# Reordering the first loads of x and of the Q and K weights in a fused attention-and-MLP kernel, with tile 0 normalised in two parts

## The chip, the cores and the metric

The kernel runs on one core of a Trainium2 chip. The metric is device microseconds of one execution; smaller is better. The profile's span (first to last instruction) is about 1.75 us shorter than that time. Runs of one call share a chip and the executions of the kernel before on it.

## The reference, cut to what matters

```python
xn = _layernorm(x)                      # x: 2048 x 640, bf16
# A: qkv = xn @ wqkv (640 x 1920), 32 heads of 20; each position attends to
#    8 positions at distance 0, 2, ..., 14; output projection wo
# B: ((xn @ w_gate) * (xn @ w_up)) @ w_down, inner width 1536
return x + A(xn, wqkv, wo) + B(xn, w_gate, w_up, w_down)
```

Rows of x are taken in 16 tiles of 128. Nothing can be multiplied before tile 0 is loaded, normalised and transposed, and the first weights are there.

## The kernel before

The kernel is written by a small list scheduler in Python. It is given tasks with priorities, keeps an assumed clock for each engine (with assumed durations and landing times), and so fixes one static order of instructions per engine. On the chip each engine then follows its order and waits for semaphores. A changed assumption about a landing can therefore reorder everything after it. The parts that matter:

```python
    # front(t): one tile of x on VectorE (dve), ScalarE (act), TensorE (pe)
    yield have("x", t)
    if t == 1:
        yield have("sd", 0)             # tile 0's square root has been planned
    for i in range(2):                  # two half-row statistics, 128x320 each
        if t == 2 and i == 1:
            yield have("xnt", 1)
        yield Task("dve", lambda: stats(i), r=[x], prio=-1 if t == 1 and i == 0 else p)
    yield Task("dve", aggr, ...)        # mean and variance
    yield Task("act", sqrt, ...)
    yield Task("dve", recip, ...)
    yield Task("dve" if t < N_DVE_A else "act", apply, ...)  # XNS = (x - mean) * rstd
    # ... transposes on PE into PSUM, then a copy to XNT (tile 0: 3 of 5 row
    # ... blocks copied by dve, 2 by act; tile 0 is followed by 3 warm-up matmuls)

    # projections of tile 0: 12 matmuls with row blocks 0-2 of the weights,
    # 8 with blocks 3-4, for Q and likewise for K; proj_group(...), cut

    x_load(0)
    # ... a small read of wqkv issued by ACT ("touch"), result not used
    x_load(1)
    wqkv_load(0, 0, 3)                  # Q weights, row blocks 0-2 (480 KB)
    wqkv_load(0, 3, NCH)                # Q weights, row blocks 3-4 (320 KB)
    x_load(2)
    wqkv_load(1, 0, 3)                  # K weights, row blocks 0-2
    wqkv_load(1, 3, NCH)                # K weights, row blocks 3-4
    x_load(3)
    warm(18)                            # matmuls on zeros until data is there
```

"Q's first rows" below are row blocks 0 to 2 of the Q weights, "Q's other rows" blocks 3 and 4; likewise for K.

Of the kernel before, what the change touches and what calls it, by code (L numbers as in the profile page):

```python
# [6 lines left out]
ALU = mybir.AluOpType  # L7
# [3 lines left out]
D = 640  # L11
NCH = 5
# [9 lines left out]
TS = 128  # L22
# [27 lines left out]
class Sched:  # L50
# [74 lines left out]
                deps[q.idx] = q  # L125
        return deps

    def op(self, eng, fn, r=(), w=(), dma=False, name="", occ=None, lat=None, lock=False, nbytes=0, mode=0, group=None, extra=0.0, acc=0.0):
        X = _Op()
        X.eng, X.fn, X.name, X.dma, X.group = eng, fn, name, dma, group  # L130
        X.needs_tick, X.event, X.pre_know, X.idx = False, None, None, len(self.ops)
        X.nth = self.n_eng[eng]
        self.n_eng[eng] += 1
        rk = [k for a in r for k in self.keys(a)]
        wk = [k for a in w for k in self.keys(a)]
        deps = self.deps_of(eng, rk, wk)
        if occ is None and not dma:
            occ = 0.1
        inorder = eng in ("pe", "act", "dve")
        start = max([self.t[eng]] + [d.end for d in deps.values()])  # L140
        if lock:
            start = max(start, self.t_lock)
        if eng == "pe" and mode != self.pe_mode:
            start += 0.1
            self.pe_mode = mode
        if dma:
            self.t[eng] = start + (0.48 if occ is None else occ)
            if acc:
                self.t_acc = max(self.t_acc, start + 3.8) + acc
                X.end = self.t_acc  # L150
            else:
                self.t_data = max(self.t_data, start + 1.2) + nbytes / 280e3
                X.end = self.t_data + 0.8 + extra
        else:
            self.t[eng] = start + occ
            X.end = start + (occ if lat is None else lat)
        if lock:
            self.t_lock = start + occ
        last = {}
        keep = []  # L160
        for d in deps.values():
            if d.dma or d.eng == "pool":
                keep.append(d)
            else:
                b = last.get(d.eng)
                if b is None or b.idx < d.idx:
                    last[d.eng] = d
        X.deps = keep + list(last.values())
        for d in X.deps:
            if not d.dma:  # L170
                d.needs_tick = True
        for k in rk:
            st = self.state.get(k)
            if st is None:
                self.state[k] = [None, [X]]
            elif inorder and st[1] and st[1][-1].eng == eng and not st[1][-1].dma:
                st[1][-1] = X
            else:
                st[1].append(X)
        for k in wk:  # L180
            self.state[k] = [X, []]
        if dma:
            if group is None or group not in self.groups:
                sem = self.nc.alloc_semaphore(f"dma{self.n_dma}")
                self.n_dma += 1
                if group is not None:
                    self.groups[group] = [sem, []]
            if group is None:
                X.event = (sem, 16)
            else:  # L190
                g = self.groups[group]
                g[1].append(X)
                X.event = (g[0], 16)
        self.ops.append(X)
        return X
# [151 lines left out]
def build_kernel(nc, A_x, A_wqkv, A_wo, B_x, B_w_gate, B_w_up, B_w_down, out):  # L347
    K = Sched(nc)
    op = K.op
# [3 lines left out]
    def sb(name, shape, dtype=BF16, at=None):  # L353
        n = mybir.dt.size(dtype)
        for s in shape[1:]:
            n *= s
        n = (n + 63) // 64 * 64
        if at is None:
            at = place[0]
            place[0] += n  # L360
        assert at + n <= 229344, (name, at + n)
        return K.sbuf(name, shape, dtype, at)
# [10 lines left out]
    NXS = 12  # L373
    XST = sb("XST", [128, NXS, D], at=a_ot + NCH * JB * 2)
# [43 lines left out]
    XNS = sb("XNS", [128, NXN, D], at=a_xr)  # L418
# [25 lines left out]
    def mark(*k):  # L444
        done.add(k)
# [4 lines left out]
    def have(*k):  # L450
        return lambda: k in done
# [4 lines left out]
    xhbm = A_x[0]  # L456
    ohbm = out[0]

    def dma(o, i, r=(), w=(), name="", eng="sp", group=None):
        n = mybir.dt.size(o.dtype)  # L460
        for s in o.shape:
            n *= s
        return op(eng, lambda e: e.dma_start(o, i), r=r, w=w, dma=True, name=name, nbytes=n, group=group)  # L463

    op("dve", lambda e: e.memset(ZERO[:], 0.0), w=[ZERO[:]], name="zero", occ=0.2)
    op("dve", lambda e: e.memset(EPSC[:], EPS), w=[EPSC[:]], name="epsc", occ=0.1)
# [3 lines left out]
       r=[IDENT[:]], w=[IDENT[:]], name="ident", occ=0.4)  # L470
# [3 lines left out]
       r=[G[:]], w=[G[:]], name="g1", occ=0.3)  # L474
    op("pool", lambda e: e.affine_select(G[:], G[:], pattern=[[-4, H]], compare_op=ALU.is_ge,
                                         fill=0.0, base=0, channel_multiplier=1),
       r=[G[:]], w=[G[:]], name="g2", occ=0.3)
    op("pool", lambda e: e.memset(KT[:, :, 0:PAD], 0.0), w=[KT[:, :, 0:PAD]], name="kpad", occ=0.3)

    def xslot(t):  # L480
        return t + 4 if t < 8 else t - 8

    def x_load(t, eng="sp"):
        dma(XST[:, xslot(t), :], xhbm[t * TS:(t + 1) * TS, :], w=[XST[:, xslot(t), :]], name=f"xld{t}", eng=eng)
        mark("x", t)

    wqkv_src = A_wqkv.rearrange("(c p) n -> p c n", p=128)

    def wqkv_load(g, lo=0, hi=NCH):
        dst = WQKV[:, WPOS[g], lo:hi, :]  # L490
        dma(dst, wqkv_src[:, lo:hi, g * D:(g + 1) * D], w=[dst], name=f"ld_wqkv{g}_{lo}")

    def loads():
        def t(f, *a):
            return Task("sp", lambda: f(*a), prio=0)

        for t_ in range(4, NXS):
            yield t(x_load, t_)
        yield t(wqkv_load, 2)
        for t_ in range(NXS, NT):  # L500
            yield have("apply", t_ - NXS)
            yield t(x_load, t_)

        def w(T, src):
            dma(T[:], src.rearrange("(c p) n -> p c n", p=128), w=[T[:]], name="ld_w")

        def pads():
            z = ZERO[:, 0:PAD].unsqueeze(1).to_broadcast([128, NCH, PAD])
            dma(vscr[:, 0:PAD].rearrange("(c p) s -> p c s", p=128), z, r=[ZERO[:, 0:PAD]], w=[("vscr", "pad")], name="vpad")

        yield have("xnt", NT - 1)
        yield t(w, WG, B_w_gate)
        yield t(pads)
        yield t(w, WU, B_w_up)
# [15 lines left out]
    def front(t):  # L530
        x, st = XST[:, xslot(t), :], STATS[:, t, 0:12]
        xs, mv = XNS[:, t % NXN, :], MV[:, t, 0:2]
        sd, rstd, nmr = SD[:, t, 0:1], SD[:, t, 1:2], SD[:, t, 2:3]
        p = 0.1 * t

        def stats(i):
            o, a = st[:, 6 * i:6 * i + 6], x[:, i * DHALF:(i + 1) * DHALF]
            op("dve", lambda e: e.bn_stats(o, a), r=[a], w=[("st", t, i)], name=f"bn{t}_{i}", occ=0.49)  # L538
# [8 lines left out]

        def recip():
            op("dve", lambda e: e.reciprocal(rstd, sd), r=[("sd", t)], w=[("rstd", t)], name=f"rstd{t}", occ=0.16)  # L549
            if t >= N_DVE_A:  # L550
                op("dve", lambda e: e.tensor_scalar(nmr, mv[:, 0:1], rstd, -1.0, op0=ALU.mult, op1=ALU.mult),
                   r=[("mv", t), ("rstd", t)], w=[("nmr", t)], name=f"nmr{t}", occ=0.13)

        def apply():
            if t < N_DVE_A:
                op("dve", lambda e: e.tensor_scalar(xs, x, mv[:, 0:1], rstd, op0=ALU.subtract, op1=ALU.mult),
                   r=[x, ("mv", t), ("rstd", t)], w=[xs], name=f"lnap{t}", occ=0.45)
            else:
                op("act", lambda e: e.activation(xs, x, ACT.Identity, bias=nmr, scale=rstd),
                   r=[x, ("nmr", t), ("rstd", t)], w=[xs], name=f"lnap{t}", occ=0.75)  # L560
            mark("apply", t)

        yield have("x", t)
        if t == 1:
            yield have("sd", 0)
        for i in range(2):
            if t == 2 and i == 1:
                yield have("xnt", 1)
            yield Task("dve", lambda: stats(i), r=[x], prio=-1 if t == 1 and i == 0 else p)
        yield Task("dve", aggr, r=[("st", t, 1)], prio=p)  # L570
        yield Task("act", sqrt, r=[("mv", t)], prio=p - 1)
        yield Task("dve", recip, r=[("sd", t)], prio=p)
# [3 lines left out]
        o = XNT[:, :, t * TS:(t + 1) * TS]  # L576
# [691 lines left out]
    N_DVE_A = 6  # L1268
# [9 lines left out]
    H_PRIO = 9  # L1278
    FIN_PRIO = 8

    x_load(0)
    tch = A_wqkv.rearrange("(c k p) n -> k c p n", k=16, c=NCH)[:, :, 0, 0:32]
    stores.append(dma(TCH[0:16], tch, w=[TCH[0:16]], name="touch", eng="act"))
    x_load(1)
    wqkv_load(0, 0, 3)
    wqkv_load(0, 3, NCH)
    x_load(2)
    wqkv_load(1, 0, 3)
    wqkv_load(1, 3, NCH)
    x_load(3)  # L1290
    K.t["act"] = 2.1
    warm(18)

# [36 lines left out]
def bass_parallel_sum__sliding_local_dilated__glu_gated_bilinear__prompt_kernel(  # L1330
    nc, A_x, A_wqkv, A_wo, B_x, B_w_gate, B_w_up, B_w_down, out
):
    build_kernel(nc, A_x, A_wqkv, A_wo, B_x, B_w_gate, B_w_up, B_w_down, out)
# [28 lines left out]
```

## Time and profile before

| | before |
|---|---|
| time, median of the first 3 runs | 270.33 us (270.25 to 270.39) |
| profiled run: time, span | 270.63 us, 268.9 us |
| TensorE (PE) busy | 262.7 us, 98% |
| first projection matmul | 7.30 us |
| first matmul after Q of tile 0 (start of the dense stream) | 9.64 us |

The first lines of the page of the kernel before: busy time by engine, then two of the rows of 40 slices (tenths of each slice busy; granted clock).

```profile
span 268.9 us, 4464 instructions
## 1 busy us (share of the span) xinstructions
PE 262.7 (98%) x1765; PEld 152.8 (57%) x1783; DVE 222.9 (83%) x282; ACT 105.4 (39%) x188; POOL 130.3 (48%) x81
...
PE   7899999999999999999999999999999999999996
...
PEclk9999999999999999999999999999999999999999
```

TensorE bounds the kernel, and only the first slices and the last are not full. The list of waits of TensorE in the kernel before (who waited for whom, us in total, times, longest) says how little there is to win. In the program's names WQKV are the Q, K and V weights, XST a tile of x as loaded, XNS the same normalised, XNT the same transposed, and PS the accumulators that TensorE writes; L640 is line 640 of the kernel:

```profile
PE PS L624 <- DVE EPSC L466: 1.3, 1, 1.3
PE PS L640 <- DVE XNT L604: 0.6, 1, 0.6
PE PS L640 <- DMA WQKV<-in_A_wqkv_dram: 0.5, 1, 0.5
PE PS L1149 <- issue: 0.3, 2, 0.2
PE PS L640 <- issue: 0.2, 1, 0.2
```

And the chain that ended last, in order of time, in its first ten microseconds (start us, length us, what), shows the order of causes in the kernel before:

```profile
1.73 5.44 DMA WQKV<-in_A_wqkv_dram
7.17 0.14 issue
7.30 0.84 PE PS L640 x12
...
8.16 0.62 PE PS L640 x8
8.78 0.29 PE PS L585 x5
...
9.09 0.50 DVE XNT L604
...
9.64 1.98 PE PS L640 x32
```

Q's first rows land at 7.17 us; the 20 matmuls of Q for tile 0 run; then come the transposes of tile 1 (L585), the copy of their result (L604), and from 9.64 us TensorE is dense. The trace also records when each of the 16 DMA engines had landed its share of a load. For Q's first rows the middle engine (the ninth of the 16 to land, here and below) was done at 5.40 us and the last at 7.17.

### The profile page before, as it was taken

The numbers are of one execution on the slowest core, as the hardware profiler recorded it, in microseconds if no ns is written. First come the engines' busy times: TensorE is split into PE (matmuls) and PEld (weight loads), VectorE is DVE, ScalarE is ACT, GpSimd is POOL, SyncE is SP. The second block draws the span as 40 slices with busy tenths as digits, with TensorE's granted clock in tenths as the row PEclk, the third lists the DMA queues.
The fourth block names the chain that finished last, engine by engine and source line by source line (L and its number), as shares of the span: only waits on it lengthen the run. The fifth ranks groups of instructions, "written<-read, shape, count | busy, mean of one in ns | idle before, by whom it ended". The sixth has DMA issues, their size and how long they took to land.

```text
span 268.9 us, 4464 instructions
## 1 busy us (share of the span) xinstructions
PE 262.7 (98%) x1765; PEld 152.8 (57%) x1783; DVE 222.9 (83%) x282; ACT 105.4 (39%) x188; POOL 130.3 (48%) x81
## 2 busy tenths in 40 slices
PE   7899999999999999999999999999999999999996
PEld 5796975444444444444444445765457654676775
DVE  4678899999999997379999899999999989992212
ACT  3369998556723232245344353024430342201000
POOL 1000000000004439900199999999999879985000
PEclk9999999999999999999999999999999999999999
DMA  6954479621414998087025953465534561022201
GB/s 206 367 188 74 98 105 339 247 97 56 142 39 113 234 244 177 0 268 151 2 52 140 240 118 79 132 176 138 152 79 130 148 195 42 27 73 61 87 28 49
DMA packets 40261, 35.58 MB, mean 132 GB/s; under 512 B 15408, under 2 KB 38448, under 8 KB 40240
## 3 DMA queue, kind: packets, MB, share of 16 engines
q1 hardware_dynamic: 39424, 33.15, 45.4%
q0 software_dynamic: 576, 2.10, 3.9%
q8 instruction: 14, 0.23, 0.4%
q10 hardware_dynamic: 240, 0.05, 0.1%
q14 instruction: 7, 0.06, 0.1%
HBM read 25.07 MB, written 5.26 MB: 113 GB/s over the span
## 4 chain that ended last, share of the span: by engine, by line
PE 94%; DMA 2%; DVE 2%; issue 1%; SPq 0%; DVEq 0%
PE PS L1149 36%; PE PS L1231 28%; PE PS L640 24%; PE PS L903 3%; DMA WQKV<-in_A_wqkv_dram 2%; PE PS L1098 2%; DVE HT L1158 1%; PE PS L585 0%; DVE RS L952 0%; DVE LOG L956 0%; SPq L463 0%; DVE XNT L604 0%; DVE SM L932 0%; DVE FOUT L1244 0%; DVEq L325 0%
## 5 line engine op out<-in xcount | busy, mean ns | idle before, releaser
L1056 POOL TENSOR_TENSOR SV<-PV 128x1024 bf16<-128x1024 f32 x40 | 93.5, 2366 | 24.7 <-DVE LOG L956 18.7
L1051 DVE TENSOR_TENSOR PV<-VX,PS 128x1024 f32<-128x1024 bf16 (+1 forms) x56 | 91.8, 1670 | 0.3 <-POOL SV L1056 0.3
L640 PE MATMUL PS<-XNT,WQKV 128*128 128x512 bf16 (+2 forms) x474 | 66.4, 299 | 1.6 <-DVE XNT L604 0.6
L1149 PE MATMUL PS<-XNT,WU 128*128 128x512 bf16 x239 | 59.6, 380 | 0.2
L1149 PE MATMUL PS<-XNT,WG 128*128 128x512 bf16 x229 | 57.3, 380 | 0.7 <-issue 0.3
L640 PEld LDWEIGHTS PS<-XNT,WQKV 128*128 128x128 bf16 x480 | 43.6, 113 | 23.8 <-DVE SD L549 1.0
L1149 PEld LDWEIGHTS PS<-XNT,WU 128*128 128x128 bf16 x240 | 23.3, 98 | 28.7 <-ACT XNT L645 0.8
L1149 PEld LDWEIGHTS PS<-XNT,WG 128*128 128x128 bf16 x240 | 23.2, 98 | 28.6 <-issue 0.8
L792 DVE TENSOR_TENSOR PRD<-QT,KT 128x2048 bf16<-128x2048 bf16 x32 | 36.8, 1217 | 0.0
L1244 DVE TENSOR_TENSOR FOUT<-PS,XR 128x320 bf16<-128x320 f32 (+1 forms) x33 | 15.7, 479 | 22.2 <-PE PS L1231 22.0
L1231 PE MATMUL PS<-WD,HT 128*128 128x320 bf16 x192 | 28.7, 300 | 0.0
L645 ACT ACTIVATE HT<-PS 128x512 bf16<-128x512 f32 x24 | 14.3, 596 | 34.0 <-PE PS L1149 34.0
L1231 PE MATMUL PS<-WO,OT 128*128 128x320 bf16 (+1 forms) x165 | 27.0, 296 | 0.0
L863 POOL TENSOR_TENSOR PRF<-PRF,PRF 128x1024 f32<-128x1024 f32 x4 | 9.4, 2352 | 33.1 <-DVE PRF L837 33.0
L1107 ACT ACTIVATE OT<-PS 128x512 bf16<-128x512 f32 x20 | 10.5, 600 | 34.4 <-PE PS L1098 34.4
L922 POOL MEMSET LOG<- 32x6 bf16 (+6 forms) x7 | 0.4, 95 | 48.4 <-ACT LOG L914 48.4
L1158 DVE TENSOR_TENSOR HT<-HT,PS 128x512 bf16<-128x512 bf16 x24 | 16.3, 680 | 8.7 <-PE PS L1149 7.0
L1231 PEld LDWEIGHTS PS<-WD,HT 128*128 128x128 bf16 x192 | 18.8, 98 | 7.6
L1231 PEld LDWEIGHTS PS<-WO,OT 128*128 128x128 bf16 x165 | 15.7, 98 | 6.6 <-issue 0.8
L837 DVE TENSOR_TENSOR PRF<-PS,KT 128x1024 f32<-128x1024 f32 x16 | 19.0, 1216 | 0.4 <-DMA PRF<-PRF 0.4
L538 DVE BATCH_NORM_STATS2 STATS<-XST 128x6 f32<-128x320 bf16 x32 | 14.7, 471 | 3.0 <-DMA XST<-in_A_x_dram 3.0
L1231 PE MATMUL PS<-WD,XNT 128*128 128x320 bf16 (+1 forms) x108 | 14.6, 285 | 0.0
(58 smaller groups left out, 216.1 us busy)
## 6 DMA issues: line engine op xcount, KB each, us to landing
VX<-v_scratch SPq DMA_DIRECT2D x80, 130.0 KB, 2.9
XST<-in_A_x_dram SPq DMA_DIRECT2D x16, 160.0 KB, 6.2
v_scratch<-VST SPq DMA_DIRECT2D x4, 640.0 KB, 4.3
XR<-in_A_x_dram SPq DMA_DIRECT2D x16, 160.0 KB, 2.9
out_dram<-FOUT SPq DMA_DIRECT2D x15, 160.0 KB, 1.8
PRF<-PRF POOLq DMA_DIRECT2D x4, 512.0 KB, 8.6
WG<-in_B_w_gate_dram SPq DMA_DIRECT2D x1, 1920.0 KB, 8.6
WU<-in_B_w_up_dram SPq DMA_DIRECT2D x1, 1920.0 KB, 12.1
```

The source lines that it names most:

```text
L538: op("dve", lambda e: e.bn_stats(o, a), r=[a], w=[("st", t, i)], name=f"bn{t}_{i}", occ=0.49)
L640: op("pe", (lambda o, l, x, c, first: lambda e: e.matmul(o, l, x, start=first, stop=(c == NCH - 1)))(o, l, x, c, first), r=[l, x], w=[o], ...
L645: X = op("act", (lambda o, i: lambda e: e.activation(o, i, ACT.Copy))(o, i), r=[i], w=[o], name=name, occ=0.12 + n * 0.9e-3)
L792: op("dve", lambda e: e.tensor_tensor(s[:], qb, kv, ALU.mult), r=[q, rk], w=[s[:]], name=f"prod{j}_{r}_{c}", occ=1.15, lock=True)
L837: X = op("dve", lambda e: e.tensor_tensor(o[:], qb, kv, ALU.mult), r=[q, rk], w=[o[:]], name=f"prow{j}_{r}_{c}_{q0}", occ=1.17)
L1051: op("dve", lambda e: e.tensor_tensor(p, vw, a, ALU.mult), r=[vv] + rk, w=[p], name=f"pv{u}_{x}_{r0}", occ=0.09 + 1.1 * nr)
L1056: X = op("pool", lambda e: e.tensor_tensor(o, p[:, :, 0, :], p[:, :, 1, :], ALU.add), r=[p[:]] + tokens(), w=[o], name=f"pva{u}_{x}", occ= ...
L1107: X = op("act", (lambda o, b: lambda e: e.activation(o, PS[:, b, :], ACT.Copy))(o, b), r=[PS[:, b, :]], w=[o], name=f"oev{u}", occ=0.58)
L1149: op("pe", (lambda l, x, c: lambda e: e.matmul(PS[:, b, :], l, x, start=(c == 0), stop=(c == NCH - 1)))(l, x, c), r=[l, x], w=[PS[:, b, :] ...
L1158: X = op("dve", lambda e: e.tensor_tensor(h, h, PS[:, hold[1], :], ALU.mult), r=[h, PS[:, hold[1], :]], w=[h], name=f"h{m}_{j}", occ=0.65)
L1231: op("pe", (lambda l, x, i: lambda e: e.matmul(dst, l, x, start=(i == 0), stop=(i == n - 1)))(l, x, i), r=[l, x], w=[PS[:, b, :]], name=f" ...
L1244: X = op("dve", lambda e: e.tensor_tensor(o, PS[:, b, 0:wid], xr, ALU.add), r=[PS[:, b, :], xr], w=[o], name=f"fin{t}_{nb}", occ=0.15 + wi ...
```

## The change

The intent is to let TensorE start earlier. Q's first rows go ahead of tile 1, K's first rows ahead of tile 2. Since tile 1 then comes later, its statistics are planned behind tile 0's normalisation, which is cut into 384 and 256 columns so that the first transposes can start sooner. The new argument `land` gives the scheduler an assumed landing time; it emits no instruction.

```diff
--- before.py
+++ after.py
@@ -125,7 +125,7 @@
                 deps[q.idx] = q
         return deps
 
-    def op(self, eng, fn, r=(), w=(), dma=False, name="", occ=None, lat=None, lock=False, nbytes=0, mode=0, group=None, extra=0.0, acc=0.0):
+    def op(self, eng, fn, r=(), w=(), dma=False, name="", occ=None, lat=None, lock=False, nbytes=0, mode=0, group=None, extra=0.0, acc=0.0, land=None):
         X = _Op()
         X.eng, X.fn, X.name, X.dma, X.group = eng, fn, name, dma, group
         X.needs_tick, X.event, X.pre_know, X.idx = False, None, None, len(self.ops)
@@ -151,6 +151,8 @@
             else:
                 self.t_data = max(self.t_data, start + 1.2) + nbytes / 280e3
                 X.end = self.t_data + 0.8 + extra
+            if land is not None:
+                X.end, self.t_data = land, max(land - 0.8, self.t_data - nbytes / 280e3)
         else:
             self.t[eng] = start + occ
             X.end = start + (occ if lat is None else lat)
@@ -456,11 +458,11 @@
     xhbm = A_x[0]
     ohbm = out[0]
 
-    def dma(o, i, r=(), w=(), name="", eng="sp", group=None):
+    def dma(o, i, r=(), w=(), name="", eng="sp", group=None, land=None):
         n = mybir.dt.size(o.dtype)
         for s in o.shape:
             n *= s
-        return op(eng, lambda e: e.dma_start(o, i), r=r, w=w, dma=True, name=name, nbytes=n, group=group)
+        return op(eng, lambda e: e.dma_start(o, i), r=r, w=w, dma=True, name=name, nbytes=n, group=group, land=land)
 
     op("dve", lambda e: e.memset(ZERO[:], 0.0), w=[ZERO[:]], name="zero", occ=0.2)
     op("dve", lambda e: e.memset(EPSC[:], EPS), w=[EPSC[:]], name="epsc", occ=0.1)
@@ -480,21 +482,21 @@
     def xslot(t):
         return t + 4 if t < 8 else t - 8
 
-    def x_load(t, eng="sp"):
-        dma(XST[:, xslot(t), :], xhbm[t * TS:(t + 1) * TS, :], w=[XST[:, xslot(t), :]], name=f"xld{t}", eng=eng)
+    def x_load(t, eng="sp", land=None):
+        dma(XST[:, xslot(t), :], xhbm[t * TS:(t + 1) * TS, :], w=[XST[:, xslot(t), :]], name=f"xld{t}", eng=eng, land=land)
         mark("x", t)
 
     wqkv_src = A_wqkv.rearrange("(c p) n -> p c n", p=128)
 
-    def wqkv_load(g, lo=0, hi=NCH):
+    def wqkv_load(g, lo=0, hi=NCH, eng="sp", land=None):
         dst = WQKV[:, WPOS[g], lo:hi, :]
-        dma(dst, wqkv_src[:, lo:hi, g * D:(g + 1) * D], w=[dst], name=f"ld_wqkv{g}_{lo}")
+        dma(dst, wqkv_src[:, lo:hi, g * D:(g + 1) * D], w=[dst], name=f"ld_wqkv{g}_{lo}", eng=eng, land=land)
 
     def loads():
         def t(f, *a):
             return Task("sp", lambda: f(*a), prio=0)
 
-        for t_ in range(4, NXS):
+        for t_ in range(3, NXS):
             yield t(x_load, t_)
         yield t(wqkv_load, 2)
         for t_ in range(NXS, NT):
@@ -547,12 +549,18 @@
 
         def recip():
             op("dve", lambda e: e.reciprocal(rstd, sd), r=[("sd", t)], w=[("rstd", t)], name=f"rstd{t}", occ=0.16)
+            mark("rstd", t)
             if t >= N_DVE_A:
                 op("dve", lambda e: e.tensor_scalar(nmr, mv[:, 0:1], rstd, -1.0, op0=ALU.mult, op1=ALU.mult),
                    r=[("mv", t), ("rstd", t)], w=[("nmr", t)], name=f"nmr{t}", occ=0.13)
 
         def apply():
-            if t < N_DVE_A:
+            if t == 0:
+                for a, b in ((0, 384), (384, D)):
+                    o, i = XNS[:, 0, a:b], x[:, a:b]
+                    op("dve", (lambda o, i: lambda e: e.tensor_scalar(o, i, mv[:, 0:1], rstd, op0=ALU.subtract, op1=ALU.mult))(o, i),
+                       r=[i, ("mv", t), ("rstd", t)], w=[o], name=f"lnap{t}", occ=0.09 + (b - a) * 0.55e-3)
+            elif t < N_DVE_A:
                 op("dve", lambda e: e.tensor_scalar(xs, x, mv[:, 0:1], rstd, op0=ALU.subtract, op1=ALU.mult),
                    r=[x, ("mv", t), ("rstd", t)], w=[xs], name=f"lnap{t}", occ=0.45)
             else:
@@ -562,11 +570,13 @@
 
         yield have("x", t)
         if t == 1:
-            yield have("sd", 0)
+            yield have("apply", 0)
         for i in range(2):
-            if t == 2 and i == 1:
-                yield have("xnt", 1)
-            yield Task("dve", lambda: stats(i), r=[x], prio=-1 if t == 1 and i == 0 else p)
+            if t == 2 and i == 0:
+                yield have("apply", 1)
+            if t in (1, 2) and i == 1:
+                yield have("xnt", t - 1)
+            yield Task("dve", lambda: stats(i), r=[x], prio=p)
         yield Task("dve", aggr, r=[("st", t, 1)], prio=p)
         yield Task("act", sqrt, r=[("mv", t)], prio=p - 1)
         yield Task("dve", recip, r=[("sd", t)], prio=p)
@@ -1278,16 +1288,15 @@
     H_PRIO = 9
     FIN_PRIO = 8
 
-    x_load(0)
+    x_load(0, land=3.2)
     tch = A_wqkv.rearrange("(c k p) n -> k c p n", k=16, c=NCH)[:, :, 0, 0:32]
     stores.append(dma(TCH[0:16], tch, w=[TCH[0:16]], name="touch", eng="act"))
-    x_load(1)
-    wqkv_load(0, 0, 3)
-    wqkv_load(0, 3, NCH)
-    x_load(2)
-    wqkv_load(1, 0, 3)
-    wqkv_load(1, 3, NCH)
-    x_load(3)
+    wqkv_load(0, 0, 3, land=5.3)
+    x_load(1, land=5.5)
+    wqkv_load(0, 3, NCH, land=7.2)
+    wqkv_load(1, 0, 3, land=8.5)
+    x_load(2, land=9.0)
+    wqkv_load(1, 3, NCH, land=10.0)
     K.t["act"] = 2.1
     warm(18)
```

## The prediction

> **What bounds the kernel.** TensorE: the page gives PE 262.7 us busy of a 268.9 us span (98%), and the chain that ended last is 94% PE. The list of waits has five entries for PE matmuls: 1.3 us at the start, 0.5 us for the WQKV load, 0.6 us for the second tile's transposed copy, 0.5 us of issue. So little can be won outside the first ten microseconds. The granted clock is 1.00 in every slice.
>
> **The head before (timeline, landings).** Tile 0 of x lands at 3.20 us; its transposed copy is complete at 6.55. The first Q weights, queued behind tile 1 of x, land at 7.17, and the first projection starts at 7.30: 0.6-0.75 us lost to weights. The other Q weights land at 8.02, so Q tile 0 ends at 8.78. Tile 1's copy ends at 9.58; PE idles 0.6 us and is dense from 9.64.
>
> Of those weight landings the middle of the 16 DMA engines is done at 5.40, but one engine is 1.75 us late, and stays late for everything behind (tile 2: middle 6.74, last 8.46), after one 1280-byte packet that took 2.05 us. This agrees with the Trainium skill, "DMA: Bandwidth & Descriptors", section "Queues, rings and completion order": each engine consumes its descriptors in ring order.
>
> **What the change does.** No arithmetic, bytes or matmuls change. (1) Q's first rows move ahead of tile 1: 160 KB less in front, about 0.45 us at the 0.44-0.46 us spacing of tile landings. I estimate 6.7 us with the late packet, 5.0-5.3 without. (2) K's first rows move ahead of tile 2: also 0.45 us. (3) Tile 1 lands at 5.5 instead of 3.6, or over 7 with a late packet. (4) Tile 0's 0.45 us normalisation becomes 0.30 + 0.23 us (estimated from 0.45 for 640 columns); transposes start 0.15 us sooner. (5) Tile 1's first statistics (0.44 us) leave the gap where VectorE waited for the square root, where they were nearly free. (6) The static order of all engines is rebuilt with new assumed landing times.
>
> **On the critical path.** First projection: 7.30 to about 6.5 (bounded by tile 0's copy and three warm-up matmuls). Q tile 0 still waits for its second rows, around 7.2-8.0. Tile 1's chain (about 3.7 us from landing to copy) ends near 9.2 if it lands at 5.5; K tile 0's matmuls can fill the time before. I expect PE to be 0.6-1.0 us further on by 12 us. Later tiles don't come sooner, but V projections (25 x 216 ns per block) fill. The last SV product on POOL ends about 1.6 us before PE uses it, so the lead should survive: 0.8 us, less what the reshuffled order costs.
>
> **Prediction: 269.5 us, range 268.7 to 270.4.** Chances: faster by over 2% 0.01, within 2% 0.98, slower by over 2% 0.01.
>
> **What would show it.** First projection at 6.3-6.8 us; Q's first rows landing 0.4 us or more earlier; normalisation pieces summing to about 0.53 us; PE dense from 9.2 us or sooner; PE busy time unchanged apart from gaps.
>
> **What would make it wrong.** The late packet falling on Q's first rows or tile 1: then tile 1's copy comes after 10 us, PE idles before it, and the gain vanishes or becomes a loss of up to 1 us. Or the rebuilt order costs tenths in the softmax or product stages, where VectorE is 90% busy. Or tiles 2 to 4, paced by VectorE at about 3.07 us each, run PE dry.

## The result, and the profile after

| | before | after |
|---|---|---|
| time, median of 6 runs each | 270.29 us (269.91 to 270.39) | 269.74 us (269.50 to 269.89) |
| ratio after to before, 95% interval | | 0.9982 (0.9969 to 0.9995) |
| profiled run: time, span | 270.63, 268.9 us | 269.85, 268.1 us |
| first projection matmul | 7.30 us | 6.69 us |
| start of the dense stream | 9.64 us | 8.76 us |

The verdict is "same" at the 2% limit; the time lies in the predicted range.

The page of the changed kernel, the same rows:

```profile
span 268.1 us, 4483 instructions
## 1 busy us (share of the span) xinstructions
PE 263.9 (98%) x1783; PEld 152.8 (57%) x1783; DVE 223.1 (83%) x283; ACT 105.4 (39%) x188; POOL 130.4 (49%) x81
...
PE   7999999999999999999999999999999999999996
...
PEclk9999999999999999999999999999999999999999
```

The 1.2 us more of busy time are not more work. The trace of before lacks 18 matmul records (1765 against 1783 weight loads) that the trace of after has.

The waits of TensorE in the changed kernel:

```profile
PE PS L634 <- DVE EPSC L468: 1.3, 1, 1.3
PE PS L595 <- DVE XNS L564: 0.3, 1, 0.3
PE PS L650 <- DVE XNT L605: 0.2, 1, 0.2
```

The wait for weights is gone. Its chain in order of time:

```profile
1.73 4.12 DMA XST<-in_A_x_dram
...
5.88 0.49 DVE STATS L540
6.37 0.26 DVE XNT L605
6.63 0.41 DVE STATS L540
...
7.06 0.22 DVE MV L543
...
7.31 0.30 ACT SD L546
...
7.63 0.17 DVE SD L551
...
7.83 0.46 DVE XNS L564
...
8.34 0.45 PE PS L595 x5
8.79 3.52 PE PS L650 x60
```

The chain has changed hands. It no longer runs through Q's weights. As the query prints it, it runs from the landing of tile 1 (5.85 us) through tile 1's statistics, square root and normalisation to its transposes, and then to 60 dense matmuls. Q of tile 0 (from 6.69 us) is not on it. The 60 begin with K of tile 0, whose first rows landed at 8.71 us, so two conditions nearly coincide at 8.76 us: tile 1's transposes and K's first rows. TensorE's timeline (start us, length us, engine, line, what; in brackets the idle time before and what ended it):

```profile
8.34 0.45 PE L595 MATMUL PS<-IDENT,XNS 128*128 128x128 bf16 x5 [0.34 <-DVE XNS L564]
8.76 3.55 PE L650 MATMUL PS<-XNT,WQKV 128*128 128x128 bf16 x60
```

The modelled end of the transposes (8.79) hides which condition came last, but the starts show it. The last transpose started at 8.57 and the matmuls of a dense stretch follow each other by 0.056 us, so the next one could have started at about 8.63. It started at 8.76, 0.05 us after K's first rows had landed: they were the later of the two, by a little over 0.1 us, although the chain does not name them. The dense stream starts 0.88 us earlier and the span is 0.8 us shorter.

So far this looks like a fixed gain of 0.8 us, of which the medians show 0.55. The experiments say otherwise.

### The profile page after: what moved, and what is told of

It reads as the page before. It is cut to its first block, busy times and chain, and to the rows that moved or that the text cites. A ratio compares the mean times of both kernels' runs of the same rounds, so it can differ in the third digit from the quotient of the medians.

```text
span 268.1 us, 4483 instructions
## 1 busy us (share of the span) xinstructions
PE 263.9 (98%) x1783; PEld 152.8 (57%) x1783; DVE 223.1 (83%) x283; ACT 105.4 (39%) x188; POOL 130.4 (49%) x81
## 4 chain that ended last, share of the span: by engine, by line
PE 96%; DMA 2%; DVE 1%; SPq 0%; issue 0%; ACT 0%
PE PS L1159 39%; PE PS L1241 28%; PE PS L650 24%; PE PS L913 3%; PE PS L1108 2%; DMA XST<-in_A_x_dram 2%; PE PS L595 0%; DVE STATS L540 0%; SPq L465 0%; DVE XNS L564 0%; DVE FOUT L1254 0%; ACT SD L546 0%; DVE XNT L605 0%; DVE MV L543 0%; DVE SD L551 0%
## 5 line engine op out<-in xcount | busy, mean ns | idle before, releaser
L1159 PE MATMUL PS<-XNT,WG 128*128 128x512 bf16 x240 | 59.7, 379 | 0.0
```

The costliest lines, as they stand in the source:

```text
L1159: op("pe", (lambda l, x, c: lambda e: e.matmul(PS[:, b, :], l, x, start=(c == 0), stop=(c == NCH - 1)))(l, x, c), r=[l, x], w=[PS[:, b, :] ...
```

## The experiments

My theory at the start (A): the change gains a fixed amount, through earlier weights, and the order of the loads and that of VectorE's work only pay together. Rivals: the weights' earlier landing alone is the gain; the new static order alone is the gain; the first projection's start decides. The second call added theory B: the gain is however long one late DMA engine happens to hold up Q's first rows in the kernel before.

### First call: the halves of the change, on one chip

**b_dmaonly.** The kernel before in its old static order, with only the first eight loads issued in the new order (the order of the recorded loads is changed after planning, so that no other engine is replanned):

```diff
     K.run()
+    issue = ("xld0", "ld_wqkv0_0", "xld1", "ld_wqkv0_3", "ld_wqkv1_0", "xld2", "ld_wqkv1_3", "xld3")
+    at = [i for i, X in enumerate(K.ops) if X.name in issue]
+    by = {X.name: X for X in K.ops if X.name in issue}
+    for i, n in zip(at, issue):
+        K.ops[i] = by[n]
     K.emit(stores)
```

> The kernel before, every engine in its old order; only the eight first loads are issued in the new order. My theory (the order of the loads and the order of VectorE's work belong together): VectorE still does tile 1's first statistics ahead of tile 0's reciprocal, so it now stands until tile 1 lands at about 5.85 us; tile 0's normalisation starts near 6.5 instead of 4.9, the first projection near 8.2 instead of 7.3, and the run is 0.5 to 1.2 us slower than the kernel before. Rival (the weights' earlier landing is the whole gain): first projection earlier and the run about 0.5 us faster than before.

Measured: 272.06 us against 269.70 for the kernel before, ratio 1.0080 (1.0067 to 1.0093). Its timeline:

```profile
5.77 0.49 DVE L538 BATCH_NORM_STATS2 STATS<-XST 128x6 f32<-128x320 bf16 x1 [1.52 <-DMA XST<-in_A_x_dram]
6.18 0.15 DVE L549 RECIPROCAL SD<-SD 128x1 f32<-128x1 f32 x1
6.36 0.45 DVE L556 TENSOR_SCALAR XNS<-XST,MV,SD 128x640 bf16<-128x640 bf16 x1
...
6.87 0.71 PE L585 MATMUL PS<-IDENT,XNS 128*128 128x128 bf16 x5 [1.58 <-DVE XNS L556]
...
8.02 2.19 PE L640 MATMUL PS<-XNT,WQKV 128*128 128x128 bf16 x20
```

The mechanism is as expected: VectorE, in order, stood 1.52 us on tile 1 with tile 0's reciprocal behind it. The load order alone is a loss. But the size was missed: 2.2 us by the ratio, not 0.5 to 1.2. Compare with b_again below, the same kernel without the edit: the dense stream starts at 11.07 us instead of 8.74. Tile 0's normalisation starts 1.47 us later (6.36 against 4.89), from there to the first projection it takes 0.10 us more, and from the first projection to the dense stream 3.05 us instead of 2.29, another 0.76. That last part is TensorE at half rate: the starts of 17 of the 128-column matmuls of Q are 106 to 107 ns apart, where b_again has 55 to 57. Its clock was still low, until about 9.9 us. That the longer idle time kept it low is likely but only argued. The table by stretches of b_dmaonly (for each: length, busy us and number of instructions per engine, granted clock, DMA share, GB/s) does not show it in the clock column (PEclk), only in the counts:

```profile
core 0: us, PE busy (x) PEld busy (x) DVE busy (x) ACT busy (x) POOL busy (x), PEclk, DMA share, GB/s
...
8.00:9.00 1.00, 1.00 (x12) 0.98 (x10) 0.61 (x2) 0.21 (x2) 0.00 (x0) 1.00 1.05 367
...
12.00:14.00 2.00, 2.00 (x39) 2.00 (x38) 1.25 (x4) 0.79 (x2) 0.00 (x0) 1.00 1.07 364
```

Ten weight loads in one microsecond against 19, with the clock printed as 1.00 in both. The packed trace of this run holds no clock record at all, and the column prints 1.00 where there is none; in the first profile of before, the records begin only at 6.77 us. The Trainium skill, "TensorE: Matmul & The Clock Gate", section "Part 1: The HAM clock gate (the "warmup" mystery)", has the same two spacings (about 107 and 56 ns) and says the array clock is low until it has been busy for a while, on a window that runs freely. The traces agree on the spacings, and on a moment that varies (the window itself no run shows): with the same 18 warm-up matmuls, tile 0's transposes at 5.4 us started 0.106 to 0.107 us apart (after the first) in the first profile of before and 0.055 to 0.056 in b_again.

**a_olddma.** The converse: the changed kernel in its new static order, its first eight loads issued in the old order (the same edit with the old list):

```diff
+    issue = ("xld0", "xld1", "ld_wqkv0_0", "ld_wqkv0_3", "xld2", "ld_wqkv1_0", "ld_wqkv1_3", "xld3")
```

> The changed kernel, every engine in its new order; only the eight first loads are issued in the old order. My theory: Q's first rows land late again (5.85 to 7.2 us), K's first rows at 9.2 to 9.8 instead of 8.7, and TensorE, which now has K of tile 0 right behind tile 1's transposes, idles there; the gain is lost: 0 to 0.4 us slower than the kernel before, 0.5 us or more slower than the changed one. Rival (the new static order is what gains): still 0.4 us faster than before.

Measured: 270.37 us, ratio 1.0023 (1.0009 to 1.0037), 0.6 us slower than the kernel before on that chip, where I had expected 0 to 0.4. TensorE's waits and timeline agree with my theory: K of tile 0 stands next in its order, and it waits for K's first rows (landed 9.31 us):

```profile
8.13 0.44 PE L595 MATMUL PS<-IDENT,XNS 128*128 128x128 bf16 x5
...
9.35 3.55 PE L650 MATMUL PS<-XNT,WQKV 128*128 128x128 bf16 x60 [0.78 <-DMA WQKV<-in_A_wqkv_dram]
```

Neither half gains; each loses by itself. The rival "the static order is the gain" is out.

**a_nosplit.** Tile 0 normalised in one piece; all other engines keep their order exactly.

```diff
-            if t == 0:
+            if t < 0:
                 for a, b in ((0, 384), (384, D)):
```

> The changed kernel with tile 0 normalised in one piece of 640 columns; all other engines keep their order exactly. If the chain of the trace is right (landing of tile 1, its statistics, its transposes, dense matmuls from 8.76 us), the split is worth nothing to the total: same as the changed kernel within 0.1 us, though tile 0's transposes start 0.1 to 0.15 us later. Rival (the first projection's start decides): 0.1 to 0.2 us slower.

Measured: 269.93 us (269.64 to 270.28), ratio to before 1.0006 (0.9993 to 1.0018). The timeline of its profiled run shows where its start came from:

```profile
6.63 1.31 PE L650 MATMUL PS<-XNT,WQKV 128*128 128x128 bf16 x20 [0.45 <-DVE XNT L605]
...
9.21 3.55 PE L650 MATMUL PS<-XNT,WQKV 128*128 128x128 bf16 x60 [0.48 <-DMA WQKV<-in_A_wqkv_dram]
```

The first projection came 3.55 us after tile 0's landing (3.08), as with the split (6.69 - 3.12 = 3.57). The split gained nothing even there, because VectorE did tile 1's statistics ahead of tile 0's copy in both. This run started dense at 9.21 us because K's first rows landed only at 9.17 in it; the time says nothing beyond that. No unedited changed kernel ran in this call, so the expected "same as the changed kernel" could be compared only across calls.

**a_copyfirst.** Tile 1's first statistics moved behind tile 0's copy; other engines keep their order.

```diff
         if t == 1:
-            yield have("apply", 0)
+            yield have("xnt", 0)
```

> The changed kernel with tile 1's first statistics moved behind tile 0's copy on VectorE; all other engines keep their order exactly. In the trace that copy stood from about 5.85 to 6.29 us behind the statistics. Mine (tile 1's chain decides): first projection at 6.3 instead of 6.7 us, but tile 1's transposes at 8.3 to 8.5 as now, and the total the same within 0.1 us. Rival (first projection decides): 0.3 to 0.4 us faster than the changed kernel.

Measured: 269.79 us, ratio to before 1.0001 (0.9988 to 1.0013), span 268.1, the span of the changed kernel's first profile. Its TensorE timeline:

```profile
6.50 1.28 PE L650 MATMUL PS<-XNT,WQKV 128*128 128x128 bf16 x20
8.36 0.45 PE L595 MATMUL PS<-IDENT,XNS 128*128 128x128 bf16 x5 [0.57 <-DVE XNS L564]
8.64 3.62 PE L650 MATMUL PS<-XNT,WQKV 128*128 128x128 bf16 x60
```

Measured from tile 0's landing, the first projection came 0.27 us sooner (3.30 us after it instead of 3.57), and TensorE waited about that much longer for tile 1 (0.57 us instead of 0.34). The rival "the first projection decides" is out for the changed kernel.

The kernel before ran at 269.70 here, where it had run at 270.29, and the variants of the changed kernel were no faster than it.

### Second call: unedited kernels, and two more variants, on a second chip

**a_again**, the changed kernel unedited.

> The changed kernel unedited, to pair it with the kernel before on this chip and to see how its landings vary. In the last call the kernel before ran at 269.70, as fast as two variants of the changed kernel, where it had run at 270.29. Theory A (the gain is fixed): ratio to before 0.997 to 0.999, about 0.5 us faster. Theory B (the gain is how much one late DMA engine happens to hold up Q's first rows in the kernel before): the ratio is nearer to 1.000 where the kernel before runs at 269.7. In its trace, time follows the later of tile 1's transposes and the landing of K's first rows (8.4 to 9.2 us so far).

**b_again**, the kernel before unedited.

> The kernel before unedited. Ratio to itself 1.000. Theory B expects that its profiled run shows Q's first rows landing between 5.9 and 7.2 us and the time following that landing: near 270.6 at 7.17 (as in the first profile), near 269.7 to 269.9 at 6.0 to 6.5. Theory A: the time does not follow the landing by more than 0.2 us.

Measured: a_again 269.77 us (269.57 to 269.85) against 269.98 (269.56 to 270.20) for before, ratio 0.9992 (0.9980 to 1.0004). b_again 269.67 us, ratio to before 0.9992, that is, the same kernel differs from itself by as much. Its profiled run had a span of 268.0 us, shorter than that of the changed kernel's first profile. Its chain in order of time:

```profile
1.72 4.60 DMA WQKV<-in_A_wqkv_dram
6.32 0.14 issue
6.45 1.43 PE PS L640 x20
7.88 0.29 PE PS L585 x5
...
8.20 0.50 DVE XNT L604
...
8.74 1.98 PE PS L640 x32
```

It is the same chain as in the first profile of before, with Q's first rows landing at 6.32 instead of 7.17 us. The middle engine landed at 5.41, as before (5.40); only the latest engine was 0.91 us behind it instead of 1.77 (and here a second one was nearly as late, at 6.24, where in the first profile the last but one had landed at 5.80). Dense stream and span are about 0.9 us earlier. Theory A, a fixed gain, falls by these traces; the ratios of the pairs alone would not exclude it, since their intervals overlap. Theory B holds on this point.

**a_notouch.** The changed kernel without the small early read of wqkv:

```diff
-    tch = A_wqkv.rearrange("(c k p) n -> k c p n", k=16, c=NCH)[:, :, 0, 0:32]
-    stores.append(dma(TCH[0:16], tch, w=[TCH[0:16]], name="touch", eng="act"))
```

> The changed kernel without the small early read of wqkv that ACT issues (it is in both kernels; nothing reads its result). If that read is what takes slow first packets off the weights, Q's first rows land later than 5.4 us and the run is slower by the same amount (0.3 to 2 us). If the late packets have nothing to do with it, Q's first rows land at 5.2 to 5.4 us and the time is the same within 0.2 us.

Measured: 269.78 us (269.37 to 270.32), ratio to before 0.9996 (0.9984 to 1.0008), Q's first rows at 5.30 us. In this one trace the missing read made no landing later.

**a_x1first.** The changed kernel with tile 1 ahead of Q's first rows again (all engines replanned):

```diff
+    x_load(1, land=3.7)
     wqkv_load(0, 0, 3, land=5.9)       # and later landings adjusted
-    x_load(1, land=5.5)
...
-            yield have("apply", 0)
+            yield have("sd", 0)        # and prio -1 for the first half, as before
```

> The changed kernel with tile 1 loaded ahead of Q's first rows again, its first statistics again in the gap of tile 0's square root; tile 0 in two parts, K's first rows ahead of tile 2 as in the change (all engines replanned). My theory (tile 1's landing at 5.85 us holds the chain in the changed kernel): tile 1's transposes at 7.6 to 7.9 instead of 8.3 us, dense matmuls from about 8.6, and 0 to 0.3 us faster than the changed kernel when Q's first rows land before 6.3 us; up to 0.5 us slower when the late engine holds them until 7 us. Rival (Q's first rows ahead of tile 1 is the essential move): 0.4 us or more slower than the changed kernel, as slow as before.

Measured: 270.15 us, ratio 1.0009 (0.9997 to 1.0021). Q's first rows landed at 6.57, so Q of tile 0 ended late, tile 1's transposes started at 8.05 behind it, and the dense stream at 9.08 after 0.59 us of waiting for tile 1's copy. Both expectations allow this, so it doesn't decide between them; it shows that with tile 1 first TensorE is again at the mercy of Q's landing.

### Third call: a direct test for the kernel before, a third pair, and a candidate

**b_x2first.** The kernel before, all engines in their old order, with tile 2's load issued ahead of Q's (the edit of b_dmaonly with another list):

```diff
+    issue = ("xld0", "xld1", "xld2", "ld_wqkv0_0", "ld_wqkv0_3", "ld_wqkv1_0", "ld_wqkv1_3", "xld3")
```

> The kernel before, every engine in its old order; only tile 2's load is issued ahead of Q's two loads instead of behind them: Q's first rows land 0.45 us later by the spacing of the tiles' landings, all else the same. If the landing of Q's first rows sets the start of the dense stream in the kernel before (as two of its traces say: 7.17 with span 268.9, 6.32 with span 268.0), first projection and run are 0.35 to 0.5 us later: 0.13 to 0.19% slower than before. If their landing has slack, the same within 0.1 us.

Measured: 270.50 us against 269.80, ratio 1.0026 (1.0012 to 1.0040). In its trace Q's first rows landed at 7.27, the first projection started at 7.40, the dense stream at 9.78, and the span was 269.0:

```profile
7.40 1.51 PE L640 MATMUL PS<-XNT,WQKV 128*128 128x128 bf16 x20 [1.24 <-DMA WQKV<-in_A_wqkv_dram]
```

The middle engine's landing was 6.01, 0.6 later than before's 5.40. The run is 0.7 us slower where I expected 0.35 to 0.5; direction and path are as expected. This is the run that shows by an intervention, and clear of noise, that the kernel before gets slower when Q's first rows land later.

**a_pair**, the changed kernel once more.

> The changed kernel unedited once more, beside the kernel before on this chip: third pairing. Theory B (gain = how late Q's first rows are in the kernel before): 0 to 0.6 us faster, more where the kernel before runs above 270.2. The span is the start of the 60 dense matmuls behind tile 1's transposes plus 259.3 us, within 0.1 us (259.34, 259.30, 259.29 so far).

Measured: 269.54 us (269.50 to 269.88) against 269.80 (269.46 to 270.39), ratio 0.9994 (0.9981 to 1.0007).

**c_x1_q0late**, a candidate: the loads of a_x1first, and the transposes of tile 1 between the two parts of Q of tile 0.

```diff
+        if wide and items[0][0] == 0:
+            yield have("tr", 1)        # marked where tile 1's transposes are planned
         if wide:
             yield Task("pe", spread, ...)   # the last 8 matmuls of Q, tile 0
```

> Candidate to beat both. Loads: tile 0, tile 1, Q's first rows, Q's other rows, K's first rows, tile 2, K's other rows, tile 3; tile 0 in two parts; tile 1's first statistics in the gap of the square root; and TensorE does tile 1's transposes between the two parts of Q's tile 0 (12 and 8 matmuls), so that the 8 fill the 0.5 to 0.6 us in which it waited for tile 1's copy in the kernel before. Expected: dense from 8.3 us when Q's first rows land at 6.3, from 8.9 when at 7.2; span 267.6 to 268.2; 0.2 to 0.5 us faster than the kernel before and 0 to 0.4 us faster than the changed one. If the fill is not the point and landing alone decides, as fast as a_x1first (span 268.4).

Measured: 269.90 us, ratio 1.0007 (0.9993 to 1.0021). Q's first rows landed at 6.73; the dense stream started at 8.82. With that landing the order of the kernel before would have started at about 9.2 (6.73 + 0.13 + 2.3, an estimate from its traces), so by this estimate the fill works; but it stays behind Q's landing and does not beat the changed kernel (8.80 in a_pair, on the same chip). The 0.2 to 0.5 us over the kernel before that I had expected did not come.

### Fourth call: a direct test for the changed kernel

**a_k3late.** The changed kernel, all engines in their order, with tile 2's load ahead of K's first rows:

```diff
+    issue = ("xld0", "ld_wqkv0_0", "xld1", "ld_wqkv0_3", "xld2", "ld_wqkv1_0", "ld_wqkv1_3", "xld3")
```

> The changed kernel, every engine in its order; only tile 2's load is issued ahead of K's first rows again (as in the kernel before), so K's first rows land 0.45 us later, at 8.9 to 9.2 instead of 8.45 to 8.76, and Q's and tile 1's loads are untouched. If K's first rows are what the dense stream of the changed kernel starts on, it starts at about their landing plus 0.05 us, the span is that plus 259.3, and the run is 0.3 to 0.45 us slower than the changed kernel: 0.0005 to 0.0015 above the kernel before. If tile 1's transposes are what it starts on, it is the same as the changed kernel: 0.0006 below the kernel before.

Measured: 269.72 us (269.49 to 270.13) against 269.99, ratio 0.9993 (0.9975 to 1.0011). By time alone this says "no effect", but the trace shows why not: K's first rows landed at 8.55 us in this run, not at 8.9 to 9.2. The middle engine was later as intended (7.94 against 7.71 in the first profile of after), but the latest engine was only 0.6 us behind it, not 1.0. The dense stream started at 8.59, 0.04 after that landing, and the span was that plus 259.4 (259.3 was expected). By time the run is inconclusive on its question; the spread of the late engine is larger than the shift that I made. Its trace answers it all the same: the last transpose of tile 1 started at 8.24, so the stream could have started at about 8.30, and it started 0.3 us later, on K's first rows.

### What ties them together

In 14 profiled runs the span follows from one number, the start of the first matmul after Q of tile 0 and tile 1's transposes (the last column is taken before rounding):

| run | Q's first rows, last engine (middle) | K's first rows, last engine | dense start | span | span - dense start |
|---|---|---|---|---|---|
| before | 7.17 (5.40) | 9.80 | 9.64 | 268.9 | 259.25 |
| b_again | 6.32 (5.41) | 9.40 | 8.74 | 268.0 | 259.23 |
| b_x2first | 7.27 (6.01) | 9.52 | 9.78 | 269.0 | 259.22 |
| b_dmaonly | 5.30 (4.85) | 8.95 | 11.07 | 270.3 | 259.23 |
| after | 5.41 (4.88) | 8.71 | 8.76 | 268.1 | 259.35 |
| a_again | 5.12 (4.81) | 8.45 | 8.50 | 267.8 | 259.34 |
| a_pair | 5.35 (4.75) | 8.76 | 8.80 | 268.1 | 259.34 |
| a_nosplit | 5.35 (4.83) | 9.17 | 9.21 | 268.5 | 259.33 |
| a_copyfirst | 5.33 (4.78) | 8.38 | 8.64 | 268.1 | 259.42 |
| a_notouch | 5.30 (4.84) | 8.59 | 8.64 | 268.0 | 259.35 |
| a_k3late | 5.07 (4.79) | 8.55 | 8.59 | 267.9 | 259.36 |
| a_olddma | 6.72 (5.40) | 9.31 | 9.35 | 268.7 | 259.35 |
| a_x1first | 6.57 (5.44) | 8.80 | 9.08 | 268.4 | 259.34 |
| c_x1_q0late | 6.73 (5.59) | 8.88 | 8.82 | 268.2 | 259.35 |

Everything after the head costs nearly the same, 259.22 to 259.42 us, in all plans. Even the small difference has a pattern: 259.22 to 259.25 in the four runs with the old static order, 259.33 to 259.36 in nine with the new one or a plan made from it, and 259.42 in a_copyfirst, whose stream has a gap of 0.08 us at 9.39. So behind its dense start the new order is about 0.1 us slower. In the kernel before the dense start is the last engine's landing of Q's first rows plus 2.4 to 2.5 us (three runs: 2.47, 2.42, 2.51). In the changed kernel Q's rows land with slack, and the dense start is 0.04 to 0.05 us after the landing of K's first rows in after, a_again, a_pair, a_nosplit, a_notouch, a_k3late and a_olddma. In a_copyfirst, where K's rows came early (8.38), it is tile 1's transposes: the stream follows the last of them by 0.056 us.

## Why the prediction was right or wrong

- **The total.** Right: 269.74 us, in the range, close to the 269.5 named. That says little, because the range holds the kernel before's own 270.29 too. The first medians differ by 0.55 us, against the 0.8 that I predicted; the two later pairs have ratios 0.9992 and 0.9994, about 0.2 us, and their intervals include 1. So a gain is shown in one of three pairings. Taken together (each call's mean of before, b_again included, minus its mean of the changed kernel: 0.50, 0.15 and 0.23 us, weighted by their errors) they give about 0.26 us with a standard error of 0.06. That the first pair came close to the prediction was partly luck: in the profile that it was built on, the last engine was 1.77 us late, and in b_again 0.91.
- **What bounds it, and that only the head can gain.** Right, and sharper than I said: span minus dense start is constant to 0.2 us over 14 runs.
- **First projection at 6.3 to 6.8 us.** Right: 6.69 (6.40 to 6.69 in four profiled runs of the changed kernel or the variant without the touch).
- **Q's first rows 0.4 us or more earlier.** Right in direction, mis-sized: 1.76 us in the first pair of profiles, of which only 0.52 is in the middle engine (5.40 to 4.88), the part due to order. The rest is the late engine, which was 1.77 us behind before and 0.53 after. I had expected 6.7 us with the late packet and 5.0 to 5.3 without; it was 5.41.
- **Q's other rows keep Q waiting until 7.2 to 8.0.** Wrong. They landed at 6.68 us, before the first projection, and the 20 matmuls ran without a gap.
- **Two parts at 0.30 + 0.23 us, transposes 0.15 us sooner.** Mis-sized: the pieces took 0.38 and 0.34 us, overlapping to 0.64 in all, and the transposes started 0.43 us after the normalisation began instead of 0.51. a_nosplit shows no gain from it even at the first projection.
- **K of tile 0 fills the time before tile 1.** Wrong way round. K's first rows came after tile 1's transposes, and TensorE waited for both.
- **The reshuffled order costs a little.** Right, and small: span minus dense start is 259.25 and 259.23 in the two profiles of the unedited kernel before, and 259.34 to 259.35 in three of the unedited changed one, so about 0.1 us.
- **The step that was mis-sized** is "Q's first weights ... land at 7.17 ...: 0.6-0.75 us lost to weights". I took one profile's late engine for a property of the kernel. b_again, the same kernel, had it at 6.32, and its TensorE waited 0.3 us for weights, not 0.5. With it the term shrinks from 0.9 us of dense start (9.64 to 8.76) to nothing in the pair b_again and after (8.74 and 8.76), or 0.24 in b_again and a_again (8.74 and 8.50).
- **The late packet as the risk.** Right that it moves the result, wrong about where it falls: in the changed kernel it lands on K's first rows (0.55 to 1.3 us behind the middle engine in the six runs with the changed kernel's load order), not on Q's or tile 1's.

The change may also give a smaller dependence on the late engine, but that is not shown. The 44 timed runs of the kernel before that served as comparison span 269.24 to 270.39 us, the 16 of the unedited changed kernel 269.50 to 269.89. But six runs of a_notouch, with the changed kernel's loads and order except for the touch, span 269.37 to 270.32, and the dense start now hangs on the late engine of K's first rows instead (dense start 8.50 to 8.80 in three profiles of the changed kernel). The 44 and 16 runs were not all paired by chip; their means, 269.93 and 269.69, agree with a gain of a quarter of a microsecond.

What stays open: why one engine is late. In each of the 14 traces 7 to 14 of the 1,400 to 1,600 packets of 1280 bytes that started before 8 us took over 0.4 us, where the median is 0.055; the longest took 2.05 us, in the first profile of before, and in three traces none took over 0.7. Which packets belong to the late engine the trace does not say. Without the touch Q's first rows landed as before (a_notouch, one trace). Whether the address or the engine decides was not tried. The moment alone does not: in the eight traces in which Q's first rows are the second load, three to nine slow packets started between 2.5 and 2.95 us, and in the six in which tile 1 is second none started before 2.93. The Trainium skill, "DMA: Bandwidth & Descriptors", section "Latency and other measured facts", gives HBM access latency as 0.2 us on average and 2 us at high load; the longest packet here, 2.05 us, is of that size, but no run shows that this is its cause. That a late engine stays late fits the section "Queues, rings and completion order" of the same page (each engine consumes its descriptors in ring order): in the profile of before the last engine was 1.77, 1.74 and 1.72 us behind the middle one for Q's first rows, Q's other rows and tile 2. It then fell to 1.48 for K's first rows. That it was one and the same engine is inferred; the landings do not name it.

## What to carry to other kernels

Before you buy a wait seen in one profile, look at the spread behind it: compare the last of the 16 engines with the middle one, and profile the unedited kernel again on another chip, since a wait on a straggler is not yours to remove in full. Loads and the in-order engine that consumes them are one decision: moved alone, the loads cost 2.2 us (0.76 of it, by its profile, from TensorE's low rate) and the new order 0.6 us; together they gained 0.2 to 0.5, clear of noise in one pairing of three. When the rest of the kernel is dense, find the one moment from which the span is a constant, and judge every variant by that moment and its spread instead of by tenths of a microsecond in the total. Where two conditions nearly coincide, go by the starts of the instructions, because a chain names only one of them.

## What the Trainium skill lacked or had wrong

- "DMA: Bandwidth & Descriptors", sections "Queues, rings and completion order" and "Latency and other measured facts": no word that plain loads on the hardware queue of SP meet 7 to 14 slow packets in the first 8 us (0.4 to 2.05 us, median of all 0.055), and that the last of 16 engines is then 0.3 to 1.8 us behind the middle one for the first weights, worth 0.9 us of span between two profiles of the same kernel. (The second section's row on slower engines is put down to the software queue.)
- "TensorE: Matmul & The Clock Gate", section "Part 1: The HAM clock gate (the "warmup" mystery)": the two spacings are right (107 and 55 to 57 ns here). It warns that clock events in a trace have been unreliable; this case adds one form of that: b_dmaonly's trace has no clock record, and the profile's clock row reads 1.00 throughout a stretch at 107 ns (8 to 9 us), so the rate has to be read from the starts of the matmuls.
- The same section puts the change to full rate at around 4 us of sustained activity, give or take 0.5 us from run to run. The spread here is wider: with the same 18 warm-up matmuls from 1.27 us on, the rate rose at 4.0 us in a_k3late and at about 6.8 in the first profile of before, 2.7 and 5.5 us after the first of them. In b_dmaonly, with a gap of 1.58 us behind the warm-up, it rose only at about 9.9 us; between the first projection and the dense stream that run took 0.76 us more than b_again. Whether the gap was the reason was not tested.
- No page says whether an early small read of a weight tensor helps its later loads; here it did not (5.30 us without, 5.12 to 5.41 with).
